# Attention on one core: the first 512 keys under their own bound, and one x block by DMA transposes

## The chip, the cores and the metric

The kernel runs on one core of a Trainium2 chip. The metric is device time in microseconds (us) of a whole execution; lower is better. Engines: PE (TensorE, matmuls; PEld its weight loads), ACT (ScalarE), DVE (VectorE), POOL (GpSimd), and SP (SyncE), which here issues DMAs. A profile's span, from first to last instruction, is some 1.8 us shorter than the time of its run; places in a profile are counted from the span's start. "Same" means within 2%. All of this case lies inside 2%, so tenths of a per cent are read here with intervals, from repeated runs, each round with the kernel before beside it on the same chip.

## The reference

Multi-head attention over one sequence of 2048 rows, 448 columns, 16 heads of 28 columns each:

```python
def reference(x, wqkv, wo):                      # x (1, 2048, 448), wqkv (448, 1344), wo (448, 448), bf16
    B, S, D = x.shape
    H = 16
    Dh = D // H
    qkv = ((x @ wqkv).reshape(B, S, 3, H, Dh)).transpose(2, 0, 3, 1, 4)
    q, k, v = qkv[0], qkv[1], qkv[2]
    scores = jnp.einsum("bhqd,bhkd->bhqk", q, k) * (Dh ** -0.5)
    p = softmax(scores, axis=-1)
    o = jnp.einsum("bhqk,bhkd->bhqd", p, v)
    return o.transpose(0, 2, 1, 3).reshape(B, S, D) @ wo
```

## The kernel before

Heads are taken in 4 groups of 4, queries in 4 blocks of 512: 16 windows, each of 16 key tiles times 4 heads. That is 1024 score tiles of 128 keys by 512 queries. There is no running maximum. A score matmul has 64 contraction rows: 32 hold q and k, the other 32 hold |q| and minus 1.03 times the largest |k| of each column. The sum is a score less an upper bound of itself, so the exponential can't overflow. The price: no score can start before KMAX, the maximum over all 2048 keys of the group.

The program is one fixed order of instructions per engine. A list scheduler inside the kernel finds it when the kernel is built: operations carry a hand-set duration, a priority and constants that say how eagerly banks are taken, and the order in which they "start" in that plan is the order in which they are emitted. Each engine is given its own list in that order, and nothing in the program reorders it later. Parts of it (`...` marks cuts):

```python
# g = group, sc = key block, b = x block, hf = half of the columns; MM = planned time of a matmul
for b in range(NQC):                              # all of x by plain loads, then PE transposes
    nc.sync.dma_start(out=XS[b][:], in_=x_perm[:, b * TPC:(b + 1) * TPC, :])
...
    evo = add(Op("DVE" if hf == 0 else "ACT", 0.6 if hf == 0 else 0.905, ev, deps=[tro], ...))   # XT copies
...
red = add(Op("DVE", 0.61, lambda: nc.vector.tensor_reduce(out=KPART[g][:, sc:sc + 1], in_=ap(),
          axis=AX.X, op=ALU.max, apply_absolute_value=True), deps=[ops[-1]], prio=prio))
evs = [add(Op("ACT", 0.585, lambda pr=pr: nc.scalar.activation(out=KB[0][pr][:, cs], in_=ap(),
          func=ACT.Identity, bias=onescol[:, 0:1], scale=1.0), deps=[ops[-1], red], ...)) ...]
m = add(Op("DVE", 0.12, lambda: nc.vector.tensor_reduce(out=KMAX[g][:], in_=KPART[g][:], axis=AX.X, op=ALU.max),
        deps=kmaxop[g], ...))
...
def emit_S(n, ap):                                # a score tile
    nc.tensor.matmul(out=ap, lhsT=KB[g % 2][i // 2][a:a + 64, j * P:(j + 1) * P],
                     rhs=QB[w % NQB][i // 2][a:a + 64, :], start=True, stop=True, tile_position=(a, 0))
# either two tiles at a time to ACT ...
nc.scalar.activation(out=PTA[pslot.idx][...], in_=PA[s.idx][...], func=ACT.Exp, bias=ACT_BIAS, scale=ACT_SCALE)
# ... or one tile to DVE, POOL, DVE: two passes, a product, a last pass (start_tile)
```

The value sums collect in one PSUM bank, PO, over the 16 key tiles ("rows") of a window; after the last row of the last window comes a serial end with four stores. After the last row of the last window comes a serial end: DVE transposes the sums and takes reciprocals, multiplies, PE projects, DVE and ACT copy out, four stores. Three of the last block's four output projections are begun ahead of it on the other groups' results, nine matmuls in all, the **late sums**:

```python
def late_sums():
    def take(tq, n):
        def f(t):
            if pos[0] < NT - NTAIL or n and any(o.kind == "B" and o.acq is not None for o in static["PE"]):
                return False                      # not until all but the last NTAIL = 12 score tiles are placed
            free = [x for x in d_slots if x.free_at <= t + 1e-9]
            if not free: return False
            ...
    for n, tq in enumerate(ACCQ):
        for gg in range(G - 1):
            prev = add(Op("PE", 0.19, lambda ...: nc.tensor.matmul(out=PD[late_acc[tq]][:, 0:D], ...), kind="A", acq=take(tq, n) ...))

def try_pe(t):                                    # PE's next instruction in the plan
    # 1. a pair of score tiles for ACT, if a score buffer is free
    o = take_static(t, lambda o: o.kind == "A" and fits(o.dur, "F") or ...)   # 2. the late sums
    if o is not None:
        return o
    ...                                           # 3. scores for DVE, value rows, projections, fillers
# the end, after the plan:
norm_dve(PO[:], DT[:], DR[:], lambda hf: DEN[hf][:])      # stream transpose, reciprocal, stream transposes
for hf in range(2):
    nc.vector.tensor_tensor(out=OTL[hf][:], in0=PO[:, hf * hw:(hf + 1) * hw], in1=DEN[hf][:], op=ALU.mult)
    for tq in (2 * hf, 2 * hf + 1):
        nc.tensor.matmul(out=fb[tq], lhsT=OTL[hf][...], rhs=WO[:, g, :], start=(tq not in late_acc), stop=True)
...
```

Of the kernel before, what the change touches and what calls it, by code (L numbers as in the profile page):

```python
# [18 lines left out]
P = 128  # L19
H = 16  # L20
HP = 32
# [7 lines left out]
MARG = 1.03  # L29
# [46 lines left out]
def kernel(  # L76
# [33 lines left out]
    DI = 2  # L110
# [8 lines left out]
    QEA = 30  # L119
# [3 lines left out]
    UQ = 16  # L123
    OD = 4
# [5 lines left out]
    QPR = 100  # L130
# [8 lines left out]
    PARTU = 40  # L139
    UO = 40  # L140

    x2 = x[0]
    out_perm = out[0].rearrange("(p t) d -> p t d", t=NKT)
    x_perm = x2.rearrange("(p t) c -> p t c", t=NKT)
# [9 lines left out]
    XT = [[sb([CK, 2, QW], BF16, f"XT{b}_{hf}") for hf in range(2)] for b in range(NQC)]  # L154
# [8 lines left out]
    KB = [[sb([P, S], BF16, f"KB{b}_{pr}") for pr in range(2)] for b in range(2)]  # L163
    KPART = [sb([P, NQC], F32, f"KPART{g}") for g in range(G)]
# [33 lines left out]
    maskcol = sb([P, 1], F32, "maskcol")  # L198
    offscol = sb([P, 1], F32, "offscol")

    tc_order = ctx.enter_context(tc.manual_schedule())

    for b in range(NQC):
        nc.sync.dma_start(out=XS[b][:], in_=x_perm[:, b * TPC:(b + 1) * TPC, :])
    for (W, off) in ((WK, D), (WQ, 0)):
        nc.scalar.dma_start(out=W[:, :, 0:GW], in_=wq3[:, :, off:off + GW])
    nc.sync.dma_start(out=WV[:], in_=wq3[:, :, 2 * D:3 * D])

# [22 lines left out]
    nc.vector.tensor_scalar(out=maskm[:], in0=maskm[:], scalar1=maskcol[:, 0:1], scalar2=None, op0=ALU.mult)  # L231
    for g in range(G):
        nc.vector.memset(VA[g][:].rearrange("p j h e -> p (j h) e")[:, :, Dh:HP], 1.0)
    nc.vector.memset(WO[:], 0.0)
    for i in range(HG):
        nc.sync.dma_start(out=WO[HP * i:HP * i + Dh, :, :],
                          in_=bass.AP(wo.tensor, wo.offset + i * Dh * D, [[D, Dh], [HG * Dh * D, G], [1, D]]))
# [44 lines left out]
    def pad_w(W, WP, g, eng):  # L282
        o = WP[g][:].rearrange("p c (h e) -> p c h e", e=HP)[:, :, :, 0:Dh]
        i = W[:, :, g * GW:(g + 1) * GW].rearrange("p c (h d) -> p c h d", d=Dh)
        if eng == "DVE":
            return lambda: nc.vector.tensor_copy(out=o, in_=i)
        return lambda: nc.gpsimd.tensor_scalar(out=o, in0=i, scalar1=1.0, scalar2=None, op0=ALU.mult)

    banks8 = [PD[0][:], PD[1][:], PD[2][:], PO[:], PA[0][:, 0:QW], PA[1][:, 0:QW], PA[0][:, QW:2 * QW], PA[1][:, QW:2 * QW]]
    xt_half = {}  # L290
    warm_bank = banks8[7]
# [7 lines left out]
    for n in range(12):  # L299
        add(Op("PE", MM, lambda: warm(n), prio=5000, kind="K", elig=lambda t: 4.6 < t < 10, acq=lambda t: warm_open[0]))  # L300
    for b in range(NQC):
        xs_in = add(Op("SP", 0.01, None, prio=-2000 + b, lat=(4.7, 6.1, 7.6, 9.0)[b]))
        for hf in range(2):
            tv = banks8[2 * b + hf].bitcast(BF16)

            def tr(b=b, hf=hf, tv=tv):
                for c2 in range(2):
                    for t in range(TPC):
# [4 lines left out]
            tro = add(Op("PE", 0.55, tr, deps=[xs_in], prio=-1200 + 10 * b + hf, lat=PLAT, kind="T",  # L313
                         acq=(lambda t: not warm_open.__setitem__(0, False)) if (b, hf) == (NQC - 1, 1) else None))

            def ev(b=b, hf=hf, tv=tv):
                i = tv[0:CK, 0:2 * QW].rearrange("p (c q) -> p c q", c=2)
                if hf == 0:
                    nc.vector.tensor_copy(out=XT[b][hf][:], in_=i)
                else:  # L320
                    nc.scalar.copy(out=XT[b][hf][:], in_=i)
            evo = add(Op("DVE" if hf == 0 else "ACT", 0.6 if hf == 0 else 0.905, ev, deps=[tro], prio=-1200 + 10 * b + hf))
            xt_done[b].append(evo)
            xt_half[2 * b + hf] = evo
    for s in a_slots + d_slots + [o_slot]:
        s.free_at = 1e18

    wkin = add(Op("SP", 0.01, None, prio=-1999, lat=5.1))
    wqin = add(Op("SP", 0.01, None, prio=-1998, lat=8.3))
    wvin = add(Op("SP", 0.01, None, prio=-1997, lat=11.0))  # L330
    for (W, WP, nm, win) in ((WK, WKP, "k", wkin), (WQ, WQP, "q", wqin)):
        eng = "DVE" if nm == "k" else "POOL"
        w_ready[(nm, 0)] = add(Op(eng, 0.3 if eng == "DVE" else 1.29, pad_w(W, WP, 0, eng), deps=[win], prio=-1005 + (nm == "q")))
# [12 lines left out]
    kuse = {}  # L346
    SI = (0, 2, 1, 3)
    kmrep = {}
    kmaxop = {}
    kmax_op = []  # L350
# [5 lines left out]
    def chain_mm(n, fn, deps, prio, elig, acq):  # L356
        ops = []
        for k in range(n):
            o = add(Op("PE", MM, (lambda k=k: fn(k)), deps=deps if k == 0 else [ops[-1]], prio=prio + 0.001 * k, kind="B",
                       elig=elig, acq=acq if k == 0 else None, lat=0.0 if k < n - 1 else PLAT))  # L360
            ops.append(o)
        return ops

    k0_bank = [(PD[0][:], 0), (PD[2][:], 2), (PO[:], 3), (PA[1][:, QW:2 * QW], 7)]

    def task_K(g, sc):
        due = g * 4 * WT - 200 + 36 * sc
        if g == 0:
            task = {"slot": None, "ap": k0_bank[sc][0]}
            acq = lambda t: xt_half[k0_bank[sc][1]].done(t)  # L370
            elig = None
            prio = -1000 + 10 * sc + 15
# [5 lines left out]
        def ap():  # L378
            return task["ap"] if "ap" in task else bank(task)[:]
        ops = chain_mm(CC, lambda cc: nc.tensor.matmul(out=ap(), lhsT=WKP[g][:, cc, :], rhs=XT[sc][cc // 2][:, cc % 2, :],  # L380
                                                       start=(cc == 0), stop=(cc == CC - 1)),
                       xt_done[sc] + [w_ready[("k", g)]], prio, elig, acq)
        cs = slice(sc * QW, (sc + 1) * QW)
        if g == 0:
            red = add(Op("DVE", 0.61, lambda: nc.vector.tensor_reduce(
                out=KPART[g][:, sc:sc + 1], in_=ap(), axis=AX.X, op=ALU.max, apply_absolute_value=True),
                deps=[ops[-1]], prio=prio))
            evs = [add(Op("ACT", 0.585, lambda pr=pr: nc.scalar.activation(
                out=KB[0][pr][:, cs], in_=ap(), func=ACT.Identity, bias=onescol[:, 0:1], scale=1.0),
                deps=[ops[-1], red], prio=prio + 0.1 * pr, lat=0.17,  # L390
                acq=(lambda t: quse and quse[0].end is not None) if sc == NQC - 1 else None)) for pr in range(2 if sc == 0 else 1)]
            kuse[sc] = evs + [red]
            for i in range(HG):
                kev[(g, sc, i)] = evs[min(i // 2, len(evs) - 1)]
        else:
            ev = add(Op("DVE", EVK, lambda: nc.vector.tensor_scalar(
                out=KB[g % 2][0][:, cs], in0=ap(), scalar1=onescol[:, 0:1], scalar2=None, op0=ALU.add),
                deps=[ops[-1]], prio=prio - 1000, elig=elig))
# [7 lines left out]
    def task_kmax(g):  # L406
        due = g * 4 * WT - 40
        prio = -945 if g == 0 else due - 1000
# [4 lines left out]
        kmax_op.append(m)  # L413
        deps = []
        c0 = 1 if g == 0 else 0
# [13 lines left out]
        if g == 0:  # L429
            for i in range(HG):  # L430
                st = SI[i] ^ 1
                kmrep[(g, 0, i)] = add(Op("DVE", 0.36, (lambda i=i, st=st: nc.vector.tensor_scalar(
                    out=KB[0][i // 2][HP * st:HP * (st + 1), 0:QW], in0=maskm[HP * SI[i]:HP * (SI[i] + 1), :],
                    scalar1=KMAX[g][HP * SI[i]:HP * (SI[i] + 1), 0:1], scalar2=None, op0=ALU.mult)),
                    deps=[m, kev[(0, 0, i)]], prio=prio + 0.1 + 0.01 * i,
                    elig=None if i < 2 else lambda t: qev[(0, 0, 1)][0].end is not None))
        nk = add(Op("DVE", 0.2, lambda: nc.vector.tensor_scalar(
            out=NK[g][:], in0=maskm[:, 0:P], scalar1=KMAX[g][:, 0:1], scalar2=None, op0=ALU.mult), deps=[m], prio=prio + 0.2,
            elig=elig if g else lambda t: qev[(0, 0, 3)][0].end is not None))
        for i in (2, 3, 0, 1):  # L440
            o = add(Op("SP", DISS + 0.07, (lambda i=i: rep_out(i, c0)), deps=[nk] + ([deps[i]] if i < 2 else []),
                       prio=due + (0.005 if i > 1 and g == 0 else 0.3) + 0.001 * i, lat=DLAT + 0.6))
# [7 lines left out]
    def task_Q(g, c):  # L450
# [4 lines left out]
        if w == 0:  # L455
# [3 lines left out]
            prio = -950  # L459
        else:  # L460
# [3 lines left out]
            prio = due - (QPR if w > 3 else 0)  # L464
        ap = lambda: bank(task)[:]
        ops = chain_mm(CC, lambda cc: nc.tensor.matmul(out=ap(), lhsT=WQP[g][:, cc, :], rhs=XT[c][cc // 2][:, cc % 2, :],
                                                       start=(cc == 0), stop=(cc == CC - 1)),
                       xt_done[c] + [w_ready[("q", g)]], prio, elig, acq)
        qb = QB[w % NQB]

        def evac(pr):
            nc.vector.tensor_scalar(out=qb[pr][:], in0=ap(), scalar1=YSC, scalar2=offscol[:, 0:1], op0=ALU.mult, op1=ALU.add)
        if w == 0:
            e0, e1 = [add(Op("ACT", 0.585, lambda pr=pr: nc.scalar.activation(
                out=qb[pr][:], in_=ap(), func=ACT.Identity, bias=offscol[:, 0:1], scale=YSC), deps=[ops[-1]], prio=-1100 if pr == 0 else -950, lat=0.17))
                for pr in range(2)]
            quse.extend([e0, e1])
            for i in range(HG):
                st = SI[i]
                o = add(Op("DVE", 0.22, (lambda i=i, st=st: nc.vector.tensor_scalar(  # L480
                    out=qb[i // 2][HP * (st ^ 1):HP * ((st ^ 1) + 1), :].bitcast(U16),
                    in0=qb[i // 2][HP * st:HP * (st + 1), :].bitcast(U16), scalar1=0x7FFF, scalar2=None, op0=ALU.bitwise_and)),
                    deps=[(e0, e1)[i // 2]], prio=-939 + 0.01 * i,
                    elig=None if i < 2 else lambda t: kmax_op[0].end is not None))
                qev[(g, c, i)] = [o]
            return
        ev = add(Op("DVE", EVK, lambda: evac(0), deps=[ops[-1]], prio=prio - 1000,
                    elig=elig if w < NQB else (lambda t: pos[0] >= (w - NQB + 1) * WT)))
# [3 lines left out]
            deps=[ev] + qmoved[n], prio=prio - 1000, kind="sb"))  # L492
        mvs = {}
        for st in (1, 3):
            mvs[st] = add(Op("SP", DISS, (lambda st=st: nc.sync.dma_start(
                out=qb[1][HP * st:HP * (st + 1), :], in_=qb[0][HP * st:HP * (st + 1), :])),
                deps=[ev], prio=prio - 100 + 0.1 * st, lat=QLAT))
# [563 lines left out]
```

## Time and profile before

| | kernel before |
|---|---|
| time, median of the runs beside the changed kernel | 414.75 us (414.62 to 414.89) |
| busy share ACT, DVE, PE, POOL | 97%, 95%, 88%, 54% |
| first exponential starts, last one ends | 16.38, 405.56 |
| first DVE pass of a tile | 17.35 |
| tail: last exponential's end to the end of the span | 7.54 |
| tiles on ACT (pairs), on DVE | 848 (424), 176 |

The stages and the start are shown in the prediction (columns of the start: start, busy us, engine, line, operation, out<-in, count; in brackets an engine's idle time and its releaser). Here is the timeline of the kernel before around its last value row (columns: start, busy us, engine, line, operation, out<-in, count; in brackets an engine's idle time and its releaser):

```profile
405.61 0.39 PE L764 MATMUL PO<-PTA_145,VA_110 128*32 128x512 bf16 x2
405.93 0.36 PE L664 MATMUL PD_202<-WO,OT_3_114 128*128 128x448 bf16 x1
...
406.04 0.72 DVE L643 STREAM_TRANSPOSE DT<-PO 128x512 f32<-128x512 f32 x1
...
406.89 0.35 PE L664 MATMUL PD_200<-WO,OT_3_122 128*128 128x448 bf16 x1
```

The last value row (L764 into PO) starts on PE as soon as the last exponential is out; the stream transpose follows 0.43 us later. Six of the late sums (L664) run from 405.93 to 407.24, after that row, beside DVE's transposes: they cost nothing there. The other three stood at 399.52 to 400.79, among other work.

### The profile page before, as it was taken

What the parts mean: (1) busy time and instruction counts of PE and PEld (TensorE: products, weight loads), DVE (VectorE), ACT (ScalarE), POOL (GpSimd) and SP (SyncE); (2) the same over time, 40 slices, a digit from 0 to 9 for tenths busy, and PEclk for the clock granted to TensorE, in tenths of its full rate; (3) what the DMA queues carried; (4) which work ended last, traced back from release to release, by engine and by line L of the source; (5) the groups of instructions that cost most, each with busy time, mean ns of one, the idle gap of its engine ahead of it and who ended that gap; (6) DMA issues with size and microseconds to landing.
All of it is one profiled execution on the core that took longest, in us unless ns stands there. A gap on an engine that the chain in (4) does not pass through costs nothing.

```text
span 413.1 us, 7525 instructions
## 1 busy us (share of the span) xinstructions
PE 362.4 (88%) x2605; PEld 121.4 (29%) x2617; DVE 394.0 (95%) x696; ACT 400.0 (97%) x439; POOL 224.1 (54%) x203
## 2 busy tenths in 40 slices
PE   8988989898898889888898988979898888989995
PEld 4533232223232232322223222222322222222231
DVE  6899999999999999999999999999999999999975
ACT  4999999999999999999999999999999999999994
POOL 2155456464655556475465656547375656556450
PEclk9999999999999999999999999999999999999999
DMA  8410011202201001110400001010310101001012
GB/s 256 77 20 21 3 47 11 53 25 54 72 1 44 2 28 30 20 38 8 111 8 27 21 9 40 2 36 11 77 48 2 47 2 35 12 27 47 4 69 89
DMA packets 33413, 15.83 MB, mean 38 GB/s; under 512 B 26016, under 2 KB 30304, under 8 KB 33376
## 3 DMA queue, kind: packets, MB, share of 16 engines
q1 hardware_dynamic: 32304, 15.05, 14.5%
q8 instruction: 20, 0.33, 0.4%
q10 hardware_dynamic: 1072, 0.32, 0.3%
q14 instruction: 17, 0.14, 0.1%
HBM read 7.37 MB, written 1.96 MB: 23 GB/s over the span
## 4 chain that ended last, share of the span: by engine, by line
ACT 86%; issue 8%; PE 2%; DMA 2%; DVE 1%; SPq 0%; DVEq 0%; ACTq 0%
ACT PTA_131 L903 5%; ACT PTA_132 L903 4%; ACT PTA_133 L903 4%; ACT PTA_136 L903 4%; ACT PTA_135 L903 4%; ACT PTA_134 L903 4%; ACT PTA_145 L903 4%; ACT PTA_140 L903 4%; ACT PTA_139 L903 4%; ACT PTA_138 L903 4%; ACT PTA_137 L903 4%; ACT PTA_144 L903 4%; ACT PTA_142 L903 3%; ACT PTA_143 L903 3%; ACT PTA_141 L903 3%
## 5 line engine op out<-in xcount | busy, mean ns | idle before, releaser
L714 POOL TENSOR_TENSOR DG_181<-DV_175,DU_169 128x512 f16<-128x512 f16 x30 | 34.6, 1155 | 34.8 <-DVE DV_175 L711 34.6
L714 POOL TENSOR_TENSOR DG_182<-DV_176,DU_170 128x512 f16<-128x512 f16 x30 | 34.6, 1155 | 28.8 <-DVE DV_176 L711 28.7
L714 POOL TENSOR_TENSOR DG_184<-DV_178,DU_172 128x512 f16<-128x512 f16 x29 | 33.5, 1155 | 29.5 <-DVE DV_178 L711 28.2
L714 POOL TENSOR_TENSOR DG_186<-DV_180,DU_174 128x512 f16<-128x512 f16 x29 | 33.5, 1155 | 26.9 <-DVE DV_180 L711 26.7
L714 POOL TENSOR_TENSOR DG_185<-DV_179,DU_173 128x512 f16<-128x512 f16 x29 | 33.5, 1155 | 25.7 <-DVE DV_179 L711 25.6
L714 POOL TENSOR_TENSOR DG_183<-DV_177,DU_171 128x512 f16<-128x512 f16 x29 | 33.5, 1156 | 22.9 <-DVE DV_177 L711 22.7
L631 PEld LDWEIGHTS <-KB_1_94 64*128 64x128 bf16 x256 | 20.8, 92 | 48.4 <-issue 47.4
L631 PEld LDWEIGHTS <-KB_0_91 64*128 64x128 bf16 x256 | 20.5, 92 | 45.8 <-issue 42.1
L631 PEld LDWEIGHTS <-KB_1_92 64*128 64x128 bf16 x256 | 20.1, 93 | 45.8 <-issue 44.0
L631 PEld LDWEIGHTS <-KB_0_93 64*128 64x128 bf16 x256 | 20.3, 92 | 43.5 <-issue 42.5
L903 ACT ACTIVATE PTA_140<-PA_199 128x1024 bf16<-128x1024 f32 x18 | 22.4, 1247 | 0.0
L903 ACT ACTIVATE PTA_144<-PA_199 128x1024 bf16<-128x1024 f32 x18 | 22.4, 1245 | 0.0
L903 ACT ACTIVATE PTA_143<-PA_198 128x1024 bf16<-128x1024 f32 x18 | 22.3, 1241 | 0.0
L903 ACT ACTIVATE PTA_142<-PA_199 128x1024 bf16<-128x1024 f32 x18 | 22.3, 1239 | 0.0
L903 ACT ACTIVATE PTA_141<-PA_198 128x1024 bf16<-128x1024 f32 x18 | 22.3, 1236 | 0.0
L903 ACT ACTIVATE PTA_139<-PA_198 128x1024 bf16<-128x1024 f32 x17 | 21.1, 1241 | 0.0
L708 DVE TENSOR_SCALAR DU_171<-PD_202 128x512 f16<-128x512 uint16 x29 | 19.8, 682 | 1.0 <-PE PD_202 L631 0.7
L708 DVE TENSOR_SCALAR DU_172<-PD_200 128x512 f16<-128x512 uint16 x29 | 19.7, 681 | 0.9 <-PE PD_200 L631 0.9
L711 DVE SCALAR_TENSOR_TENSOR DV_178<-PD_200,DU_172 128x512 f16<-128x512 uint16 x29 | 19.8, 684 | 0.3
L711 DVE SCALAR_TENSOR_TENSOR DV_176<-PD_201,DU_170 128x512 f16<-128x512 uint16 x29 | 19.8, 683 | 0.2
L708 DVE TENSOR_SCALAR DU_169<-PD_200 128x512 f16<-128x512 uint16 x29 | 19.8, 682 | 0.2 <-PE PD_200 L631 0.2
L903 ACT ACTIVATE PTA_145<-PA_198 128x1024 bf16<-128x1024 f32 x16 | 20.0, 1247 | 0.0
(596 smaller groups left out, 1511.3 us busy)
## 6 DMA issues: line engine op xcount, KB each, us to landing
RRB_194<-SCR_196 SPq DMA_DIRECT2D x8, 256.0 KB
RRB_195<-SCR_197 SPq DMA_DIRECT2D x7, 256.0 KB
KB_1_94<-KB_0_93 SPq DMA_DIRECT2D x4, 128.0 KB
XS_127<-in_x_dram SPq DMA_DIRECT2D x1, 448.0 KB
XS_128<-in_x_dram SPq DMA_DIRECT2D x1, 448.0 KB
XS_129<-in_x_dram SPq DMA_DIRECT2D x1, 448.0 KB
XS_130<-in_x_dram SPq DMA_DIRECT2D x1, 448.0 KB
out_dram<-XS_127 SPq DMA_DIRECT2D x1, 448.0 KB
```

Of the source, the lines that this page charges most:

```text
L631: nc.tensor.matmul(out=ap, lhsT=KB[g % 2][i // 2][a:a + 64, j * P:(j + 1) * P], rhs=QB[w % NQB][i // 2][a:a + 64, :], start=True, stop=Tru ...
L708: p1 = add(Op("DVE", P1, lambda: nc.vector.tensor_scalar(out=DU[b][:], in0=lo, scalar1=SIG / 65536, scalar2=SIG * (SS - 0.5), op0=ALU.mult ...
L711: p2 = add(Op("DVE", P1, lambda: nc.vector.scalar_tensor_tensor(out=DV[b][:], in0=lo, scalar=65536 * (SS - 0.5 + CE / C3), in1=DU[b][:], o ...
L714: gq = add(Op("POOL", PTT, lambda: nc.gpsimd.tensor_tensor(out=DG[b][:], in0=DV[b][:], in1=DU[b][:], op=ALU.mult), deps=[p2], prio=n, kind ...
L903: nc.scalar.activation(out=PTA[pslot.idx][:, 0:len(ns) * QW], in_=PA[s.idx][:, 0:len(ns) * QW], func=ACT.Exp, bias=ACT_BIAS, scale=ACT_SCALE)
```

## The change

The intent is to start the exponentials before all of x has been projected. For the first two query blocks (NF = 2), the first 512 keys (FB = 4 key tiles) are taken first, under a bound that those keys alone give: 32 early score tiles that need only the first block of x. Their value sums are written out, multiplied by a factor exp(difference of the two bounds), and added to the sums over the other 1536 keys. WQ loads earlier and its padding moves to ACT; one XT copy is split between ACT and DVE; the last block of x comes by four DMA transposes instead of a plain load, sixteen PE transposes and two copies. Seven scheduling constants change and many new ones are added; smaller edits (the bound's margin from 1.03 to 1.03125, a later load of `wo`, memsets moved to POOL) are not shown. The core of the diff (cuts marked `...`):

```diff
-    DI = 2
+    DI = 1
-    QEA = 30
+    QEA = 20
-    UQ = 16
-    OD = 4
+    UQ = 30
+    OD = 2
-    QPR = 100
+    QPR = 50
-    PARTU = 40
-    UO = 40
+    PARTU = 50
+    UO = 20
+    FB = TPC
+    NF = 2
...
+    XT3 = 14.0
+    XBAR = True
+    KENG = ('ACT', 'DVE', 'DVE', 'ACT')
+    HENG = ('ACT', 'ACT', 'ACT', 'DVE')
...
+    if XBAR:
+        for cc in range(CC):
+            nc.sync.dma_start(out=XT[NQC - 1][cc // 2][:, cc % 2, :],
+                              in_=bass.AP(x.tensor, x.offset + cc * CK, [[D, QW], [1, P]]), transpose=True)
...
+            if b == 0 and hf == 1 and XSP:
+                evo = add(Op("ACT", 0.48, lambda ev=ev: ev(eng="ACT", c1=1), deps=[tro], prio=-4999))
+                xt_done[b].append(evo)
+                evo = add(Op("DVE", 0.36, lambda ev=ev: ev(eng="DVE", c0=1), deps=[tro], prio=-4999))
...
+    tbank = (((PD[0][:], None), (PD[1][:], None)), ((PD[2][:], None), (PA[0][:, 0:QW], None)),
+             ((PO[:], None), (PA[0][:, QW:2 * QW], None)), ((PD[2][:], 2), (PO[:], 3)))
...
-                and kmrep[(g, j // TPC, i)].done(t))
+                and (w < NF and j < FB or kmrep[(g, j // TPC, i)].done(t)))
...
+    def task_factor(w):
...
+        e = add(Op("ACT", 0.49, lambda: nc.scalar.activation(out=RRB[w][:], in_=bank(task)[:], func=ACT.Exp, scale=ACT_SCALE),
+                   deps=[m], prio=0))
...
+    def finish_block(w):
+        pvop = rows[(w, FB - 1)]["pv"]
+        ev = add(Op("DVE", 0.62, lambda: nc.vector.tensor_copy(out=OSB[w][:], in_=PO[:]), deps=[pvop], prio=-5000))
...
+        first_part[w] = [add(Op("POOL", 1.22, lambda: nc.gpsimd.tensor_tensor(out=OSB[w][:], in0=OSB[w][:], in1=RRB[w][:], op=ALU.mult),
+                                deps=[ev, factor[w]], prio=-10, kind="n"))]
...
-        if acts and fits(MM, "S") and pos[0] < NT - NTAIL and s_ready(pos[0], t) and d_inflight[0] < ND + (OD > 0):
+        if acts and not starved and (not TW or kmax_op[0].end is not None) and fits(MM, "S") and ...
```

The last line keeps DVE's tiles behind the full KMAX (TW = 1).

## The prediction

> **What bounds the kernel now.** I read the page first (busy shares, then the chain that ended last), then busy time by stage, then the start in order of time. The page:
>
> ```profile
> PE 362.4 (88%) x2605; PEld 121.4 (29%) x2617; DVE 394.0 (95%) x696; ACT 400.0 (97%) x439; POOL 224.1 (54%) x203
> ...
> ACT 86%; issue 8%; PE 2%; DMA 2%; DVE 1%; SPq 0%; DVEq 0%; ACTq 0%
> ```
>
> ScalarE (ACT) and VectorE (DVE) are both near full, and the chain that ends last is ACT for 86%. The 1024 score tiles of 128x512 are shared: ACT takes exponentials two tiles at a time (L903), DVE with POOL makes the others from a cubic (L708, L711, L727; POOL between). Does an engine wait anywhere? The stages, in busy microseconds:
>
> ```profile
> core 0: us, PE busy (x) PEld busy (x) DVE busy (x) ACT busy (x) POOL busy (x), PEclk, DMA share, GB/s
> 0.00:4.73 4.73, 3.48 (x8) 1.09 (x8) 2.85 (x18) 1.28 (x1) 1.49 (x11) 1.00 0.63 180
> 4.73:9.56 4.83, 4.45 (x56) 3.54 (x56) 2.96 (x6) 2.46 (x3) 0.81 (x1) 1.00 1.06 338
> 9.56:14.21 4.65, 4.49 (x33) 2.47 (x32) 3.36 (x5) 4.02 (x6) 0.52 (x1) 1.00 0.68 102
> 14.21:16.38 2.17, 2.12 (x13) 0.82 (x12) 1.97 (x7) 1.85 (x4) 0.00 (x0) 1.00 0.00 0
> 16.38:18.55 2.17, 2.10 (x26) 1.26 (x24) 2.08 (x7) 1.94 (x2) 0.00 (x0) 1.00 0.38 91
> 18.55:405.56 387.01, 343.23 (x2470) 111.34 (x2478) 377.32 (x650) 387.01 (x423) 221.23 (x191) 1.00 0.13 30
> 405.56:413.10 7.54, 2.56 (x12) 0.87 (x11) 3.44 (x8) 1.40 (x3) 0.00 (x0) 0.89 0.34 122
> ```
>
> From 18.55 to 405.56 ACT is busy for 387.01 of 387.01 us: no wait in that stage can be removed. Only three things can move the end: how early the exponentials start, how much other work ACT and DVE do, and the tail of 7.54 us. The change works on the first. The start:
>
> ```profile
> 4.73 1.19 PEld L311 LDWEIGHTS <-XS_127 128*112 128x112 bf16 x16 [0.82 <-DMA XS_127<-in_x_dram]
> ...
> 6.11 1.01 ACT L321 COPY XT_1_64<-PD_201 112x1024 bf16<-112x1024 bf16 x1 [3.11 <-PE PD_201 L311]
> ...
> 8.75 1.33 POOL L287 TENSOR_SCALAR WQP_75<-WQ 112x448 bf16<-112x448 bf16 x1 [6.38 <-DMA WQ<-in_wqkv_dram]
> ...
> 10.93 1.00 ACT L321 COPY XT_1_70<-PA_199 112x1024 bf16<-112x1024 bf16 x1
> 11.83 0.70 ACT L388 ACTIVATE KB_1_92<-PD_200,onescol 128x512 bf16<-128x512 f32 x1
> 12.42 0.69 ACT L388 ACTIVATE KB_0_91<-PD_202,onescol 128x512 bf16<-128x512 f32 x1
> ...
> 14.21 0.16 DVE L410 TENSOR_REDUCE KMAX_99<-KPART_95 128x1 f32<-128x4 f32 x1
> 14.29 0.69 ACT L474 ACTIVATE QB_0_85<-PD_201,offscol 128x512 bf16<-128x512 f32 x1 [0.24 <-PE PD_201 L466]
> ...
> 15.92 0.39 PE L631 MATMUL PA_198<-QB_0_85,KB_0_91 64*128 64x512 bf16 x2
> ...
> 16.38 1.02 ACT L903 ACTIVATE PTA_131<-PA_198 128x1024 bf16<-128x1024 f32 x1 [0.25 <-PE PA_198 L631]
> ```
>
> The first block of x is in SBUF at 4.73, but the first exponential starts at 16.38, because each score row needs a bound from the largest key over all 2048 keys (KMAX at 14.21), hence all of x, four transposes, four K projections. ACT is not idle meanwhile: from 6.11 it copies XT halves and evacuates K and Q almost back to back. So starting sooner does not make those jobs vanish, it only lets exponentials go between them.
>
> **What the skill says.** "Perfetto Trace Analysis", Optimizing Scalar/DVE Operations: the profiled time of a Scalar or DVE instruction holds a part that overlaps the next one. The trace agrees: an exponential lasts 1.02 to 1.29 us, but 423 of them fill 387.01 us, 0.915 each; a DVE pass lasts 0.68 but follows the last after 0.60; a K evacuation on ACT lasts 0.69 with 0.58 between starts. I count with spacings. "DMA: Bandwidth & Descriptors", Latency and other measured facts, gives DMA transposes an effective 261 GB/s; "Advanced Engine Details and Errata", X-Bar Transpose (TRN2), calls them as fast as regular DMAs. At 261 GB/s the 459 KB would be an estimated 1.8 us. The trace of before has no such transfer. The changed kernel's own schedule plans with more: SP occupied 8.5 us, the last block there at 14.0 (before, the plain load of that block let PE start on it at 9.23). "VectorE: DVE Perf Modes", Why PSUM operands drop a tier: PSUM sources lose the fast mode. Agrees: a Q evacuation from PSUM takes 0.74, the 128x512 sign mask in SBUF 0.28.
>
> **The change part by part.**
> 1. *When exponentials can start.* The new chain needs the first block alone. XS at 4.73; its two transposes are done at about 6.1 as now; the second XT copy is split between ACT and DVE, done at about 6.7 instead of 7.12. The WQ load moves ahead of the second x block (it gated POOL at 8.75), so I take it as landed by 6; its padding goes to ACT (0.45 by the kernel's schedule). K0 and Q0 matmuls: last halves about 6.8 to 7.9 (0.60 per pair of matmuls, 0.22 apart). ACT: K0 to 8.1, Q0 to 8.75. DVE meanwhile reduces K0 (0.69), then mask 0.20, copy 0.20, two bounds of 0.35 and a handoff: 9.9 to 10.2. Scores to exponential takes 0.46 (15.92 to 16.38). First exponential at about 10.7, that is 5.7 us earlier.
> 2. *ACT work pushed behind that start.* Before 10.7 fit WQ padding, the half copy, K0 twice, Q0, one XT copy (about 3.6 us of work in the 4.6 us from 6.1). Left over: one XT copy 0.90, K3 0.58, two new exponentials for the rescaling factors 2 x 0.58: 2.6 us. In all ACT gets easier: formerly four copies and seven evacuations, 4 x 0.90 + 7 x 0.58 = 7.7; now 2.5 x 0.90 + 4 x 0.58 + 0.45 + 1.16 = 6.2. Start bubbles stay (now 0.23, then one buffer of two is opened late): I leave 0.4 on each side. ACT gains 5.7 - 2.6 = 3.1 us.
> 3. *DVE.* It may not start tiles before the full KMAX in the new order. With the last block at 14.0, K3, reduce and KMAX end about 16; first tile at about 17, as now (17.35). On top come two evacuations for the split value sums (2 x 0.60) and two multiplications by the block's bound (2 x 0.20); the four 0.35 us bound copies, the last XT copy leave the start, two K evacuations and eight bounds enter it, filling DVE's idle time there. I take a loss of 1.0 us.
> 4. *POOL*: two more products of 1.2 us on an engine at 54%: hidden. *PE*: small factor matmuls: hidden. *SP queue*: moves and bound fills for keys 512 to 2047 land by an estimated 23. The 32 early tiles alone would keep ACT until 10.7 + 16 x 0.915 + 2.6 = 28, so this is covered.
> 5. *Sum.* The schedule shares tiles, so a gain on one engine is spread. Rates: ACT 2/0.915 = 2.19 tiles per us, DVE 1/(3 x 0.60) = 0.56, together 2.74 to 2.75. (2.19 x 3.1 - 0.56 x 1.0) / 2.75 = 2.3 us. Tail unchanged: same windows, same final chain, four 112 KB stores. Several scheduling constants are retuned; I credit 0.3 us. 414.77 - 2.6 = **412.2 us**.
>
> **Rivals.**
> *The transposing DMA comes late.* Engines run a fixed order, planned for 14.0. If the data lands at 17, PE stands at K3 with scores queued behind it and ACT idles up to 3 us: the gain is gone, 415. For it: no transpose in the trace to check, and a 1.99 us issue of four small loads shows SP is slow. Against: the early tiles leave slack after K3, and the planned 14.0 already is five times the skill's figure, so somebody measured it.
> *The full 5.7 us arrives.* If all ACT leftovers fall into unavoidable gaps (one score buffer is shut until XT copies are done, leaving ACT about 0.46 per round), ACT gains up to 5 and DVE nothing: 2.19 x 5 / 2.75 = 4.0, 410.5; with good retuning 409.5.
> *DVE becomes the bound.* The rescaling puts 1.6 us and more on an engine already 95% busy, and DVE waits for KMAX. If it starts at 20, the loss is 3.7 x 0.56/2.75 = 0.8 us: 413.
> *PE cools down* in the emptier start: the granted clock is 1.00 in every stage now, with filler matmuls up to the first scores; those are kept, so I give it little.
>
> **Range and chances.** The mechanism is sound and bounded: at most 5.7 of 414.77 us is 1.4%, under 2% even if nothing were given back. A fall over 2% needs 8.3 us, more than the transposes can plausibly lose. Range 409.6 to 414.9; faster 0.02, same 0.96, slower 0.02.
>
> **What would show it.** First L903-type exponential near 10.7 (step 1 right if 10.2 to 11.5); ACT work other than exponentials after it 2.6 us (step 2); first DVE pass 16.5 to 18 (step 3); ACT pairs down and DVE tiles nearly unchanged from 176, or up by a few if it is rebalanced; transposes landed by 14 and PE not waiting on them; ACT busy without gap from about 20 to the last exponential near 403; tail 7.5 us. The prediction is wrong if ACT shows gaps between 11 and 28, if K3 waits on the DMA, or if the tail changes.

## The result, and the profile after

Ratios here are the mean time of one kernel's fast runs over that of the other's of the same rounds, so not quite the ratio of the medians quoted.

| | before | after | predicted |
|---|---|---|---|
| time, median | 414.75 (414.62 to 414.89) | 415.62 (415.37 to 415.72) | 412.2 (409.6 to 414.9) |
| ratio, 95% interval | | 1.002 [1.0006, 1.0034] | |
| first exponential | 16.38 | 12.66 | 10.7 |
| first DVE pass | 17.35 | 21.65 | 16.5 to 18 |
| last exponential ends | 405.56 | 404.13 | about 403 |
| tail | 7.54 | 9.47 | 7.5 |
| ACT pairs, DVE tiles | 424, 176 | 425, 174 | down, about 176 |

The class "same" was right and the direction wrong: 0.2% slower, outside the range. The page of the changed kernel, busy shares and the chain that ended last:

```profile
PE 358.8 (87%) x2597; PEld 119.9 (29%) x2608; DVE 394.7 (95%) x699; ACT 399.1 (97%) x439; POOL 225.4 (55%) x217
...
ACT 85%; PE 7%; issue 6%; DVE 1%; ACTq 0%
```

The shares hardly moved. PE's share of the chain rose from 2% to 7%, a hint that something on PE stands on the path, but no more than that: the kernel of experiment 1 below, with the tail mended, still has 5%. The stages (same columns as before), cut at the first and last exponential:

```profile
0.00:12.66 12.66, 9.70 (x68) 5.54 (x69) 7.71 (x29) 6.26 (x8) 3.92 (x26) 1.00 0.94 201
12.66:404.13 391.47, 345.71 (x2505) 113.14 (x2515) 383.68 (x664) 391.47 (x429) 221.52 (x191) 1.00 0.14 32
404.13:413.60 9.47, 3.39 (x28) 1.19 (x26) 3.32 (x8) 1.41 (x4) 0.00 (x0) 0.91 0.27 97
```

ACT is busy 391.47 of 391.47 us: the mechanism works, no gap anywhere. Exponentials start 3.72 us earlier and the last one ends 1.43 us earlier. Where the rest went can be counted. The earlier start brings 3.72, and a gap of 0.33 after the first exponential of the kernel before (its second started at 17.63, 1.25 after the first, where 0.92 is the spacing) is gone. Against that, ACT does a K evacuation (0.58) and two factor exponentials (0.48 each, by their spacing) after the start, and one more pair (0.915), since DVE now makes 174 tiles: 3.72 + 0.33 - 1.54 - 0.92 = 1.6, measured 1.43. Then the tail gives back more than that: 9.47 - 7.54 = 1.93.

The tail of the changed kernel:

```profile
403.74 1.88 PE L827 MATMUL PD<-WO,OT 128*128 128x448 bf16 x9
...
405.54 0.39 PE L963 MATMUL PO<-PTA,VA 128*32 128x512 bf16 x2
...
405.77 0.82 PE L963 MATMUL PO<-PTA,VA 128*32 128x512 bf16 x12
406.64 0.72 DVE L806 STREAM_TRANSPOSE DT<-PO 128x512 f32<-128x512 f32 x1 [2.20 <-PE PO L963]
```

All nine late sums (L827, 1.88 us in one block) now stand **ahead** of the last four value rows (L963, 16 matmuls from 405.54 to 406.59), and DVE's stream transpose waits 2.20 us for those rows. The last exponential was out at 404.13. In the plan the late sums come before value rows as soon as PSUM banks are free for them (step 2 of `try_pe`); for the second and third projection no other projection may still be waiting for a bank. DVE's last tile, which frees such a bank, now ends at 403.38 instead of 400.82. That this is why the plan chose the new order is read from the code, not tested.

The start, on ACT and then on DVE:

```profile
6.83 0.59 ACT L383 COPY XT<-PD 112x512 bf16<-112x512 bf16 x1 [0.93 <-DVE XT L381]
8.59 0.78 ACT L480 ACTIVATE KB<-PD,bndcol,selcol 128x512 bf16<-128x512 f32 x1 [1.18 <-PE PD L464]
...
10.87 1.92 ACT L383 COPY XT<-PA 112x1024 bf16<-112x1024 bf16 x2
12.66 6.59 ACT L1107 ACTIVATE PTA<-PA 128x1024 bf16<-128x1024 f32 x7
19.25 0.69 ACT L489 ACTIVATE KB<-PO,onescol 128x512 bf16<-128x512 f32 x1
```

```profile
9.40 0.69 DVE L471 TENSOR_REDUCE KPART<-PD 128x1 f32<-128x512 f32 x1 [2.61 <-ACT KB L480]
...
20.69 0.16 DVE L511 TENSOR_REDUCE KMAX<-KPART 128x1 f32<-128x4 f32 x1
...
21.65 0.68 DVE L905 TENSOR_SCALAR DU<-PD 128x512 f16<-128x512 uint16 x1
```

On PE, the first scores and the last K projection (K3):

```profile
11.39 0.66 PE L794 MATMUL PA<-QB,KB 64*128 64x512 bf16 x2 [0.69 <-DVE QB L618]
...
18.82 0.39 PE L464 MATMUL PO<-XT,WKP 112*128 112x512 bf16 x1
```

ACT's half of the split XT copy waits 0.93 us for DVE's copy out of the same PSUM bank, and DVE's reduce of K0 waits for ACT's evacuation of the same bank. Two XT copies (1.92 us) run on ACT before the first exponential. DVE is nearly full from 9.40 to 21.65 (11.05 of 12.25 us), with bounds, masks, copies, evacuations and reduces, and KMAX comes at 20.69 (14.21 before).

### The profile page after: what moved, and what is told of

Read it like the earlier page. It is cut to its first block, busy times and chain, and to the rows that moved or that the text cites. A ratio compares the mean times of both kernels' runs of the same rounds, so it can differ in the third digit from the quotient of the medians.

```text
span 413.6 us, 7537 instructions
## 1 busy us (share of the span) xinstructions
PE 358.8 (87%) x2597; PEld 119.9 (29%) x2608; DVE 394.7 (95%) x699; ACT 399.1 (97%) x439; POOL 225.4 (55%) x217
## 3 DMA queue, kind: packets, MB, share of 16 engines
HBM read 6.91 MB, written 1.96 MB: 21 GB/s over the span
## 4 chain that ended last, share of the span: by engine, by line
ACT 85%; PE 7%; issue 6%; DVE 1%; ACTq 0%
ACT PTA L1107 83%; PE PA L794 2%; PE PO L963 1%; PE PA L354 1%; ACT XT L383 1%; PE PD L827 0%; ACT KB L480 0%; PE PD L794 0%; ACT RRB L846 0%; ACT OUTF L1236 0%; PE PD L744 0%; DVE XT L381 0%; PE PO L663 0%; PE PO L744 0%; PE PD L370 0%
## 5 line engine op out<-in xcount | busy, mean ns | idle before, releaser
L1107 ACT ACTIVATE PTA<-PA 128x1024 bf16<-128x1024 f32 x425 | 390.5, 1250 | 0.0
L911 POOL TENSOR_TENSOR DG<-DV,DU 128x512 f16<-128x512 f16 x174 | 200.5, 1155 | 170.1 <-DVE DV L908 168.8
L794 PE MATMUL PA<-QB,KB 64*128 64x512 bf16 x850 | 167.6, 380 | 44.8 <-ACT PTA L1107 42.1
L794 PEld LDWEIGHTS <-KB 64*128 64x128 bf16 x1024 | 66.7, 93 | 187.1 <-issue 178.9
L905 DVE TENSOR_SCALAR DU<-PD 128x512 f16<-128x512 uint16 x174 | 117.4, 680 | 3.1 <-PE PD L794 2.9
L908 DVE SCALAR_TENSOR_TENSOR DV<-PD,DU 128x512 f16<-128x512 uint16 x174 | 118.0, 682 | 1.3
L924 DVE SCALAR_TENSOR_TENSOR PTD<-PD,DG 128x512 uint16<-128x512 f32 x174 | 118.2, 680 | 1.1 <-POOL DG L911 0.9
L963 PE MATMUL PO<-PTA,VA 128*32 128x512 bf16 x850 | 85.5, 386 | 0.0
L794 PE MATMUL PD<-QB,KB 64*128 64x512 bf16 x174 | 64.7, 376 | 1.4 <-DVE PTD L924 0.6
L963 PE MATMUL PO<-PTD,VA 128*32 128x512 bf16 x174 | 55.7, 386 | 0.0
L963 PEld LDWEIGHTS <-VA 128*32 128x32 bf16 x1024 | 18.8, 94 | 47.5 <-issue 47.2
L1068 PE MATMUL PO<-zrow,zeros 128*128 128x512 bf16 x29 | 10.7, 387 | 0.2 <-issue 0.2
```

The lines of the kernel that those rows point to most:

```text
L905: p1 = add(Op("DVE", P1, lambda: nc.vector.tensor_scalar(out=DU[b][:], in0=lo, scalar1=SIG / 65536, scalar2=SIG * (SS - 0.5), op0=ALU.mult ...
L908: p2 = add(Op("DVE", P1, lambda: nc.vector.scalar_tensor_tensor(out=DV[b][:], in0=lo, scalar=65536 * (SS - 0.5 + CE / C3), in1=DU[b][:], o ...
L911: gq = add(Op("POOL", PTT, lambda: nc.gpsimd.tensor_tensor(out=DG[b][:], in0=DV[b][:], in1=DU[b][:], op=ALU.mult), deps=[p2], prio=n, kind ...
L924: f = add(Op("DVE", P1, lambda: nc.vector.scalar_tensor_tensor(out=PTD[st["s"].idx][:].bitcast(U16), in0=PX[slot.idx][:], scalar=EBITS + C ...
L963: nc.tensor.matmul(out=PO[HP * st:HP * (st + 1), :], lhsT=VA[g][:, j, st, :], rhs=r["p"][i][1](), start=first, stop=last, tile_position=(0 ...
L1068: nc.tensor.matmul(out=PO[:], lhsT=zeros[:], rhs=zrow[:], start=first, stop=first, skip_group_check=True)
```

## The experiments

Theory **A**: the early start works, and the tail's order throws its gain away. Rival **B**: the tail is long because DVE's tiles end later (403.38), so any order would give it. Further questions: what holds the start (bank waits?), what DVE's late start costs, and whether the transposes, the second block and the constants pay. All kernels but those of experiments 2 and 5 hold the tail fix of the first, so they are compared with that one (413.18) and with the kernel before of their own rounds. "Kernel 1", "kernel 3" and "kernel 4" are those of experiments 1, 3 and 4.

### 1. The late sums after the last value row

```diff
-                if pos[0] < NT - NTAIL or n and any(...):
+                if pos[0] < NT - NTAIL or pv_next[0] < NROW or n and any(...):
```

> The changed kernel with one edit: the nine late matmuls of the output projection (L827) may be placed on PE only after the last row of value sums. Nothing before the last 2 us of exponentials moves. Theory A (the change's early start does pay, 1.4 us at the last exponential, and is given back because those nine matmuls now stand ahead of the last four rows): last exponential still ends at about 404.1, the first stream transpose (L806) starts at about 404.8 instead of 406.64, time 1.7 to 1.9 us below the changed kernel, 413.7 to 413.9, so about 1 us faster than before. Rival B (the tail is long because DVE's last tile is late, 403.38 instead of 400.8, and the value rows have to wait for it): the transpose still starts near 406, less than 0.5 us is won.

Measured: 413.18 us (413.17 to 413.67), before 414.78; ratio 0.9966 [0.9953, 0.9978]. Its tail:

```profile
403.58 0.82 PE L963 MATMUL PO<-PTA,VA 128*32 128x512 bf16 x12
...
404.34 1.88 PE L827 MATMUL PD<-WO,OT 128*128 128x448 bf16 x9
404.46 0.72 DVE L806 STREAM_TRANSPOSE DT<-PO 128x512 f32<-128x512 f32 x1 [0.27 <-PE PO L963]
```

The same nine matmuls take the same 1.88 us, now beside DVE's work. The stretch of exponentials is as long as in the changed kernel (12.40 to 403.87, again 391.47 us), the tail is 7.53 us. DVE's last tile ends at 403.12 in a run that started 0.26 earlier than the changed kernel's (there 403.38), so it is as late as ever, and B falls and A is confirmed: the order of the tail is worth 1.94 us, more than the changed kernel's early start had won. The 0.26 us are not the edit's: in the profiled runs of four other kernels with the same order at the start (experiments 2, 6 with DVE held, and the last two of 8) the exponentials begin at 12.38 to 12.78, so a start read from one run is good to some 0.4 us only. **This version is faster than both kernels.**

### 2. One constant of the changed kernel back: DI

```diff
-    DI = 1
+    DI = 2
```

> Undoes one constant of the change: DI back from 1 to 2, so output-projection matmuls are favoured over score rows near the end only while two cubic tiles are in flight. In the order that is emitted only the last few us differ: three of the nine late matmuls come early, six after the last value row. Theory A: same as e1 within 0.3 us, 413.7 to 414.1. Rival B: no gain, about 415.5.

Measured: 414.87 (414.71 to 415.0), ratio 1.0002 [0.9989, 1.0016]: a miss. The value rows are done at 404.57, but the plan has put another job ahead of the transpose, this time on DVE:

```profile
404.51 0.55 PE L744 MATMUL PD<-WO,OT 128*128 128x448 bf16 x2
404.91 1.16 DVE L748 TENSOR_TENSOR XS<-PD,KB 128x448 bf16<-128x448 f32 x2 [1.81 <-PE PD L744]
...
405.98 0.71 DVE L806 STREAM_TRANSPOSE DT<-PO 128x512 f32<-128x512 f32 x1
```

Two output-projection adds of the block before (L748) wait for their matmuls and hold up the transpose, which starts 1.52 us later than in kernel 1. Another order, nearly the same loss.

### 3. The first block's second XT half in a bank of its own

Fix 1, and the half that DVE copies is transposed into PO instead of sharing a bank with ACT's half.

```diff
-                        nc.tensor.transpose(out=tv[0:CK, k * P:(k + 1) * P],
+                        nc.tensor.transpose(out=(PO[:].bitcast(BF16) if (b, hf, c2) == (0, 1, 1) else tv)[0:CK, k * P:(k + 1) * P],
...                        # and the copy reads from there
```

> e1 plus one edit at the start, order of everything else unchanged: the two halves of the second XT copy of block 0 read from two PSUM banks instead of one. In the trace of the changed kernel ACT's half waits 0.93 us for DVE's half. Theory C (that wait, and not the matmuls or the weights, sets the start): ACT's half copy starts at about 6.2 instead of 6.83, K0 evacuation at about 7.9 instead of 8.59, first exponential at about 12.0 instead of 12.66, time 0.5 to 0.7 us below e1. Rival D (ACT cannot start it sooner, WQ padding or PE order sets it): first exponential unchanged within 0.2, same time as e1 within 0.2.

Measured: 413.57 (413.02 to 414.5), ratio 0.9977 [0.9964, 0.9989]: no gain over kernel 1, so theory C fails on the time. On ACT:

```profile
6.14 0.59 ACT L383 COPY XT<-PD 112x512 bf16<-112x512 bf16 x1 [0.38 <-PE PD L370]
8.02 0.78 ACT L480 ACTIVATE KB<-PD,bndcol,selcol 128x512 bf16<-128x512 f32 x1 [1.29 <-PE PD L464]
...
12.09 2.88 ACT L1107 ACTIVATE PTA<-PA 128x1024 bf16<-128x1024 f32 x3
16.20 3.95 ACT L1107 ACTIVATE PTA<-PA 128x1024 bf16<-128x1024 f32 x4 [1.23 <-PE PA L794]
```

The wait of ACT's copy for DVE is gone. The Trainium skill has this, in "PSUM — Partial Sum Buffer", section PSUM bank collisions raise a hardware error: two engines, reads included, must not be on one bank and quadrant at once, so software has to order them. The case agrees: 0.93 us of waiting in the shared bank, none for DVE here. But the first exponential moves by only 0.31 (12.40 to 12.09), which is inside the scatter of the start named above, and a gap of 1.23 us opens, in this profiled run. The stages of this kernel and, beneath, of kernel 1:

```profile
13.00:16.50 3.50, 3.31 (x10) 0.77 (x9) 2.25 (x7) 2.27 (x4) 0.00 (x0) 0.53 0.00 0
```

```profile
13.00:16.50 3.50, 3.27 (x16) 0.82 (x13) 2.68 (x7) 3.50 (x5) 0.00 (x0) 1.00 0.10 7
```

The granted clock was 0.53 here, so PE's 3.31 busy us held 10 matmuls where 3.27 hold 16. The rival that the prediction set aside, that PE cools down, does occur. It does not in every run: the fastest of the five (413.02) is 0.15 below kernel 1's fastest.

### 4. The same with filler matmuls

Kernel 3 with five matmuls on zeros into a free bank: three ahead of the first scores, one ahead of the second Q projection, one ahead of the third pair of scores.

```diff
+        if o.eng == "PE" and o.kind == "S":
+            n_s[0] += 1
+            fills = {1: 3, 3: 1}.get(n_s[0], 0)
...
+        for _ in range(fills):
+            nc.tensor.matmul(out=PD[1][:], lhsT=zeros[:], rhs=zrow[:], start=True, stop=True)
```

> e3 plus five filler matmuls on zeros in PE's gaps between 10 and 13 us (three before the first scores, one before Q1, one before the third pair), everything else in the same order. In e3 the granted PE clock fell to 0.5 from about 13 to 16.5 us and ACT stood 1.23 us. Theory G (PE does too little in the new start, so the clock falls in some runs; not the bank split itself): clock 1.00 in every microsecond from 8 to 19, no ACT gap, first exponential at about 12.1, last at about 403.5, time 412.7 to 412.9, spread of the runs under 0.5. Rival H (the gap belongs to the new order of arrivals): the gap of about 1.2 us stays, time as e3, 413.6.

Measured: 413.16 (412.94 to 413.63), ratio 0.9964 [0.9951, 0.9976]; equal to kernel 1. In the profiled run the clock stayed at 1.00 and ACT has no gap, as the theory wanted. That missing matmuls let the clock fall is not shown by this: it is one profiled run of each; kernel 1 kept its clock with PE as little busy from 10 to 14 us (2.75 us, kernel 3 has 2.74); and one run with fillers (413.63) has a mean clock of 0.995. But the first exponential is at 12.35, because another wait took the place of the bank's:

```profile
10.53 1.93 ACT L383 COPY XT<-PA 112x1024 bf16<-112x1024 bf16 x2 [0.37 <-PE PA L370]
```

These two copies stand ahead of the first exponential on ACT, and their transposes wait for the third x block, which landed at 9.39. The bank wait, seemingly 0.93 us, was worth nothing that these runs can resolve at the end.

### 5. The fillers in the changed kernel, tail as it was

> The changed kernel with only the five filler matmuls of e5, nothing else. Tells whether a fallen clock was part of the changed kernel's 415.6: three of its four runs had a mean clock of 0.994 to 0.995, the profiled one 0.998 and 415.37. Theory G: runs agree at 415.3 to 415.4 with mean clock 0.998, so the clock was worth 0.2 to 0.3 us. Rival: median stays 415.6.

Measured: 415.76 (415.17 to 415.84), ratio 1.0021. The runs fall in two groups, 415.2 at mean clocks of 0.997 to 0.998 and 415.8 at 0.994 to 0.995, as the changed kernel's own do (415.37 at 0.998; the other three 415.59 to 415.72 at 0.994 to 0.995). So the runs with lower clocks are 0.2 to 0.35 us slower in the changed kernel and 0.5 to 0.7 here. That the clock is the cause is likely, not shown; my fillers did not cure it. Where those dips fall is open: every profile I have of the changed kernel is of a run without one.

### 6. DVE held back, ACT held back

Kernel 1 with nine memsets ahead of DVE's first pass, or with four copies ahead of ACT's first exponential, order otherwise unchanged.

```diff
+        if o.eng == "DVE" and o.dur == P1 and o.lat == SEM and not held:
+            held.append(1)
+            for _ in range(9):
+                nc.vector.memset(DUM[:], 0.0)
```

> e1 with nine dummy memsets of about 0.27 us (2.4 us in all) put on DVE just before its first cubic pass, order unchanged. It measures what a later DVE start costs when the order is fixed. Theory J (the weights of the prediction: a DVE microsecond is worth 0.2 of the total): time up 0.5 us. Rival K (with a fixed order DVE's lateness passes through the score banks and the value rows to PE and ACT): up 1.5 to 2.4 us, with ACT gaps soon after 24 us.

> e1 with four dummy copies of about 0.6 us (2.4 us in all) put on ACT just before its first exponential, order unchanged. ACT is gapless, so both views expect nearly the full 2.4 us: last exponential 2.3 us later, time 415.4 to 415.7. If it is under 1.5 us, ACT has hidden slack at the start.

Measured, DVE: 416.8 (416.68 to 417.74), ratio 1.0058. The nine memsets took 3.41 us, more than the 2.4 planned. The time rose by 416.8 - 413.18 = 3.6, about as much as the delay. ACT, which the delay does not touch, gets a gap:

```profile
29.73 1.02 ACT L1108 ACTIVATE PTA<-PA 128x1024 bf16<-128x1024 f32 x1 [2.74 <-PE PA L795]
```

and on PE:

```profile
28.16 0.37 PE L795 MATMUL PD<-QB,KB 64*128 64x512 bf16 x1 [2.56 <-DVE PTD L925]
...
28.79 0.91 PE L795 MATMUL PA<-QB,KB 64*128 64x512 bf16 x2
```

PE's order is fixed; scores for ACT (28.79) stand in it behind a score for DVE that waits for DVE's bank (28.16). So the weight that I gave DVE (0.56/2.75, a fifth of a delay) does not hold under a fixed order; whether it holds where the plan is made anew with the delay known was not tested. Measured, ACT: 418.01 (417.71 to 418.14), +4.8 for 2.5 us of copies, far over what was expected. Neither is a clean rate: the clock fell as well, to 0.50 from 29 to 32 in DVE's profiled run, after PE had stood for those 2.56 us, and to 0.50 from 17 to 19 in ACT's, with a gap of 1.15 us after. What the clock added is not separated.

### 7. No DMA transposes

Kernel 1 with the last x block by plain load and PE transposes (`XBAR = False`), a path that the changed source holds but does not use.

> e1 with the last x block loaded plainly and transposed on PE again (two more PSUM copies, both on DVE), schedule made anew. Theory E (the DMA transposes are hidden, PE never waits on them, and they take 1.3 us of copies off DVE): first cubic pass about 1.2 us later than in e1 (22.8), time 0.3 to 1.0 us above e1. Rival F (the 7.35 us of DMA issue cost more than they save): time below e1, KMAX earlier than 20.7.

Measured: 417.5, with a **wrong result** (relative error 0.44): by my reading that path overwrites a PSUM bank before it has been read. So its banks were mended (cut), and the result became correct:

```diff
-             ..., ((PD[2][:], 2), (PO[:], 3)))
+             ..., ((PD[1][:], -1), (PO[:], 4)))     # -1: wait for the Q0 evacuation
-    k0_wait = [lambda: [xt_half[0]], lambda: quse, ...]
+    k0_wait = [lambda: [xt_half[0]], lambda: quse + [xt_half[6]], ...]
```

> e4 gave a wrong result, because the path without DMA transposes reuses a PSUM bank too early; here the last block's two transposes go to a free bank and wait for it, rest as e1, schedule made anew. Theory E (DMA transposes pay because they take two copies of 0.68 off DVE and two transposes off PE at the start): last exponential 1.0 to 3.0 us after e1's 403.86 and time 414.2 to 416.2. Rival F (they only shift waiting): last exponential within 0.5 of e1's.

Measured: correct, 417.36 (417.12 to 417.75), ratio 1.0059 [1.0046, 1.0072], 4.2 us above kernel 1. DVE's first pass comes at 22.77 instead of 21.38, the last exponential ends 2.9 us later, and the rest is again a tail with adds ahead of the transpose (it starts at 408.61). The kernel with the transposes is the faster one; how much of the 4.2 us is theirs is not settled, since the plan after the start differs too.

### 8. One early block instead of two; the old constants; a tail constant

```diff
-    NF = 2
+    NF = 1
+    open_when(d_slots[2], [xt_half[2]])
```

> e1 with only one query block taking the first 512 keys early (NF 2 to 1), schedule made anew. The bound over all keys is ready at about 20.7 and its fills by about 27. One block gives 16 tiles, 8 exponentials of 0.915 us, so ACT would run dry at about 12.4 + 7.3 + 0.6 = 20.3. Theory L (two blocks are needed to cover the wait for the full bound): ACT gaps of 4 to 7 us between 20 and 28, time 416.5 to 420. Rival M (other work or DVE tiles fill it): gaps under 2 us, within 1 us of e1.

Measured: 420.24 (420.10 to 420.46), ratio 1.0126. ACT has gaps of 5.7 us in all, one of them 3.60 us ahead of the exponential at 25.62, waiting for scores: 16 early tiles do not cover the wait for the full bound, 32 do.

Kernel 1 with all seven constants of the kernel before:

```diff
-    DI = 1; QEA = 20; UQ = 30; OD = 2; QPR = 50; PARTU = 50; UO = 20
+    DI = 2; QEA = 30; UQ = 16; OD = 4; QPR = 100; PARTU = 40; UO = 40
```

> e1 with the seven scheduling constants that the change also retuned set back (DI 2, QEA 30, UQ 16, OD 4, QPR 100, PARTU 40, UO 40), schedule made anew. Theory N (the retuning is not decoration; the order falls into a worse place without it): the start up to 25 us as in e1 within 0.2, but DVE idle later on and the last exponential 2 to 4 us after e1's 403.86, time 415 to 417.5. Rival: constants matter under 0.5 us, time 413.2 to 413.7.

Measured: 419.09 (418.38 to 420.67), ratio 1.0105, 5.9 us above kernel 1, more than expected. The start is the same (12.78); ACT waits once, 2.5 us, for scores between 89 and 92; the last exponential ends at 407.76, 3.9 later, and the transpose starts 1.87 later still (0.59 in kernel 1).

Kernel 1 with one constant that sets when the out-projections become urgent:

```diff
-    UO = 20
+    UO = 10
```

> e1 with UO 20 to 10: the out-projection of the window before last becomes urgent later, so DVE's last tiles end sooner. A try at a better tail. Expect last exponential as in e1, DVE's last pass about 0.8 us earlier, time 0 to 0.3 us below e1, 412.9 to 413.2; over 413.5 would say that the tail's order is sensitive beyond the matmuls moved in e1.

Measured: 414.83 (414.52 to 416.5), ratio 1.0003. The last exponential ends at 403.87 exactly as in kernel 1, and 1.6 us are lost in the median all the same (1.34 between the profiled runs). Of these 1.31 stand in the tail: an add of the projections (L748) at 405.23, which waited 1.96 us for its matmul, stands on DVE ahead of the stream transpose, which starts at 405.77 instead of 404.46.

## Why the prediction was right or wrong

**What bounds the kernel: right.** ACT is gapless in the changed kernel too, so only the start, the amount of work and the tail could move the end.

**Step 5, "Tail unchanged: same windows, same final chain": wrong, and the largest error.** The final chain is the same, but its start does not hang on the last exponential alone. It hangs on where a fixed order puts nine matmuls, of which six used to lie after the last value row and three well before it. The tail measured 9.47 us instead of 7.54, and moving only those nine gave 7.53. Of the 3.4 us between 412.2 and 415.62 this is 1.93. The prediction lists a changed tail as a sign of being wrong, but has no cost and no rival for it.

**Step 1, first exponential at about 10.7: 2 us too early** (12.66). Two terms make this up. The first scores began at 11.39, where the prediction has 10.24 (10.7 - 0.46): K0, which I had evacuated by 8.1, began its evacuation only at 8.59, and even with the bank wait gone at 8.02, since the projections' matmuls ended later than I had put them. That is 1.15. And I expected one whole XT copy on ACT ahead of the first exponential; there were two, and ACT is free only at 12.66, 1.27 after the scores began instead of 0.46. That is 0.8. The skill's page on PSUM would have told of the bank wait, but in kernels 3 and 4 undoing it moved nothing at the end.

**Step 2, 2.6 us of ACT work pushed behind the start: 1.54**, the counterpart of the same second copy: what had run before the start had not to run after it. ACT's gain by this account is 3.72 + 0.33 - 1.54 = 2.5, where I had 3.1.

**Step 3, DVE's first pass at about 17: 21.65.** I waited for KMAX, and got that from the transposes' landing, with K3, its reduce and KMAX done at about 16. In the run K3's last matmul ended only at 19.21, since it stands in PE's order behind other projections and score pairs, and DVE took its reduce at 19.96, behind its own work, which fills 9.40 to 21.65. I had added up neither. A loss of 1.0 us was put down for DVE; by the start alone it is 4.3 late, and one pair more went to ACT. The three steps together left the last exponential at 404.13, about 1.2 us later than the sum of the prediction has it (405.56 - 2.6 = 402.96).

**Step 4, POOL, PE and SP hidden: right** as far as the changed kernel shows (ACT never waits). **Retuning, 0.3 us: far too small.** Without it kernel 1 is at 419.09, 5.9 us worse. The constants are part of the change, not a finish on it.

**The rivals.** The transposing DMA did not come late: in the changed kernel's trace no wait of PE at K3 is put down to it, and the kernel without it took 4.2 us more. (The prediction's "five times the skill's figure" fits the planned 8.5 us on SP, 8.5/1.8 = 4.7, and not 14.0, a time of landing.) DVE "becomes the bound" came true in its premise (start at 20, in fact 21.65), and its cost as put there, 0.8, was not tested for a new plan. "PE cools down" got little and did occur in variants, and probably in three of the changed kernel's four runs: about 0.25 us of the median, from the distance of its median to its run at 0.998. (The clock of the kernel before, too, was 1.00 only up to its last exponential; its tail has 0.89.) 1.93, 1.2 and 0.25 make 3.4; the 1.2 holds the scatter of one profiled start.

What stays open is where the clock dips of those runs fall, and what the transposes and DVE's late start are worth apart from the plan that each brings with it.

## What to carry to other kernels

Where an order is fixed ahead of time, an early start is worth only what the end lets through: look at the last few microseconds on every engine and ask what stands ahead of the last instruction of the chain, for work placed there can cost its full length (here 1.88 us of matmuls, 1.93 us of tail). Three different plans each lost 1.3 to 1.9 us in this way, with exponentials that ended at nearly the same time. And before crediting a start, add up the work of every engine in it: a wait that is removed (here a shared bank) often has another close behind.

## What the Trainium skill lacked or had wrong

- "TensorE: Matmul & The Clock Gate", Part 1, What's actually happening: the clock falls to half after an idle window of about 3.4 us and the window's phase varies between runs. Half is what kernel 3 shows (0.50 from 14 to 16, 0.53 on the mean of 13.00 to 16.50). But no idle window of that length precedes it: PE was busy 0.32, 0.65, 0.96 and 0.81 of the four microseconds from 10 to 14. Part 4 says that transposes do not count as busy in the same way, so those of 8.19 to 10.14 may belong to the quiet stretch; that is not tested. In the runs of experiment 6 the clock fell to 0.50 after PE had stood for 2.56 and 2.69 us, also less than 3.4. The page does not say how much activity in a window is enough. With five fillers there the clock stayed at 1.00 in the profiled run.
- "DMA: Bandwidth & Descriptors", Latency and other measured facts: it gives DMA transposes 261 GB/s, from which the prediction's 1.8 us came. The four transposes held SP's queue for 7.35 us of issuing (1.21 to 3.22 us each), and the loads behind them on that queue were issued from 10.54 on. The bandwidth may well be right for the data, but the issuing took four times as long here, and no page gives an issue time for transposes of this size, which is what planning lacks.
- "PSUM — Partial Sum Buffer", PSUM bank collisions raise a hardware error: right, and overlooked in the prediction. It does not put a number on the cost of the ordering that software must add: 0.93 us for ACT behind DVE's copy here, some 0.8 us for DVE's reduce behind ACT's evacuation (8.59 to 9.37; the rest of DVE's 2.61 idle is before the K0 matmuls ended at 8.48), and yet nothing at the end of the kernel when the first was removed.
- No page has how much an engine off the critical path delays the others in a fixed order: 3.41 us more on DVE ahead of its first pass came with 3.6 us in all, a fall of the clock included.
